# A state-space scan with a wave mixer on one core: u of two adjoining tiles with its tails as 64-row products, token weights loaded as float and cast on chip, and the written order made anew

## The chip, the cores and the metric

The kernel runs on one core of a Trainium2 chip. The metric is the device time of one execution in microseconds (us). The kernel before takes 207.25 us, the median of 3 runs (206.68 to 207.59). A run's time is somewhat longer than the span of its profile, which runs from the first to the last thing the profiler saw.

## The reference

There are two stages. The first is a recurrence over 768 steps for each of 4 batches and 8 heads, with a 40 x 40 state:

```
y[t]   = r[t] @ state
Sa     = state @ a[t]
state  = state * w[t] - outer(Sa, b[t]) + outer(v[t], k[t])
```

The second is a mixer over tokens and channels, with x the result y laid out as (batch, 768 tokens, 320 channels):

```
theta  = x @ w_theta                       # 320 x 320
zr, zi = x * cos(theta), x * sin(theta)
u      = x + w_tok_r @ zr + w_tok_i @ zi   # 768 x 768, over tokens
out    = u + relu(u @ w_ch)                # 320 x 320
```

Inputs and output are float32; the products run in bf16.

## The kernel before, in words

The tokens are cut into 24 tiles of 128 (six for each batch), numbered 0 to 23. The recurrence is done tile by tile in matrix form: within a tile it becomes products of 128 x 128 score matrices, and only the state (`gt`) is carried from tile to tile. The mixer works on the same tiles; the row products of a tile need z of all six tiles of its batch.

Every step of a tile is a short name in one long text, `ORDER`, and the kernel does nothing but walk through it: `LDK:3` issues the load of k of tile 3, `KH:3G` computes its scaled k and b on GpSimd, `PSI:3@0` makes a score matrix on TensorE into bank 0. The letter behind a step is its engine (A is ScalarE or ACT, V is VectorE or DVE, G is GpSimd or POOL, S is a transposing DMA issued by SP). Each engine executes its own steps in the order in which they stand in the text; the scheduler that inserts the waits does not reorder them. The text thus sets which buffer is held when, and what waits behind what on each engine and queue.

The steps that the texts below speak of:

- Loads: `LDW`, `LDK`, `LDB`, `LDA`, `LDV`, `LDR` (w and r come for two tiles at once). Before, k, a, b and v of the first tile or two go to ACT's queue, all others to SP's.
- Decay: `LN` takes the logarithm of w for two tiles. `CSI` and `CSE` sum it over tokens on TensorE, as products of 64 rows with a triangular mask (`pair_inc`, `pair_exc`). `INVW` and `WI` exponentiate the sums on ACT.
- Scaled inputs: `KH` (k and b by invW), `AH` (a by Wi), casts `CR`, `CV`.
- Transposes on TensorE with copies out of PSUM behind them: `TRK`/`EKBT`, `TRA`/`EAT`, `TRV`/`EVT`, `TRR`/`ERT`, `NUT`/`ENUT`, `GD`/`EGD`, `XT`/`EXT`, `UT`/`EUT`. Where the copy has the letter S, a DMA transposes from memory and TensorE does nothing.
- Scores: `PSI`, `PHI`, `LV`, `LU`, each eight products of 64 rows, two heads' halves of the array in turn. `EPSI`, `EPHI`, `ELV`, `ELU` bring them to memory: on DVE with the mask in the same instruction, on ACT without it, and then POOL masks them (`MPSI`, `MPHI`, `MLV`, `MLU`).
- `X0`, `NU`: the corrections. `GT`, `GI`, `EGA`, `EGT`: the new state. `Y`, `EX`: the result x of a tile.
- Mixer: `TH` (x by `wth`), `SIN` on ACT, `ZR` (z of a tile), `YR` (row products, twelve a tile, 320 columns each), `EU` (u), `CH` (u by `wch`), `EO` (result), `ST` (store).
- Weights over tokens: `LDT:t.n` loads 128 rows of one of the two matrices, `WT` transposes them on TensorE, `EWT` copies. `LDC` loads the channel weights.

The 320 channels are contracted in three slices of 128, of which the third holds 64 channels and 64 zeros. x and u lie in tiles of 384 columns padded with zeros for this:

```
    def mix3(dst, lhs, rhs):
        for kt in range(3):
            mm(dst, lhs[:, kt, :], rhs[:, kt, :], kt == 0, kt == 2)
```

The token weights are loaded by POOL's queue into bf16 tiles, with the conversion done by the DMA; three buffers of each matrix.

Of the kernel before, what the change touches and what calls it, by code (L numbers as in the profile page):

```python
# [19 lines left out]
LDW:0 LDK:0A LDB:0 LDA:0A LDA:1 LDB:1A LDK:1 LDV:0A LN:0A LDC:0.0G LDT:0.0G CSI:0@0 LDC:0.1G CSE:0@1 WI:0A  # L20
INVW:0A KH:0V TRK:0@0 AH:0V EKBT:0A TRA:0@3 LDW:2 EAT:0V LDR:0 KH:1V PHI:0@1 PSI:0@0
EPSI:0A MPSI:0G CV:0A LDB:2 EPHI:0A AH:1V TRK:1@1 EKBT:1V LN:2A TRA:1@2 MPHI:0G LDV:1 TRV:0@3
LDK:2 X0:0@0 EAT:1V CSI:2@0 CR:0A ENX:0V LDA:2 PSI:1@1 INVW:2A EVT:0V NU:0 ENU:0A EPSI:1V
TRR:0@1 PHI:1@0 LDB:3 ERT:0A GT:0@2 CV:1A LDK:3 CSE:2@1 EPHI:1V TRV:1@3 ERT:1A NUT:0@0 KH:2G
WI:2A EGT:0V LV:0@0 LDA:3 EVT:1V X0:1@1 ENX:1A ENUT:0A ELV:0V LDV:2 AH:2G GD:0@2 LDR:2 TRK:2@3
KH:3G LV:1@1 NU:1 EKBT:2A LU:0@0 ELV:1V LDW:4 TRA:2@0 ENU:1A LDV:3 ELU:0A NUT:1@3 AH:3G EAT:2V
GT:1@1 ENUT:1V PSI:2@1 TRK:3@0 EGD:0V EPSI:2V LDK:4 LDA:4 GI:1 EKBT:3A CV:2G TRA:3@3 LU:1@0
ELU:1A CR:2G PHI:2@1 EGT:1V X0:2@2 EAT:3V EPHI:2V MLU:0G ENX:2A LN:4A LDB:4 TRR:2@0 PSI:3@0
LDR:4 CV:3G PHI:3@1 MLU:1G Y:0@1 EPSI:3A MPSI:3G EPHI:3V NU:2 TRV:2@3 CSE:4@0 LDV:4 ENU:2A
ERT:2A EVT:2V GT:2@2 EX:0V WI:4A AH:4G CSI:4@1 INVW:4A Y:1@3 LDW:6 NUT:2@1 EGA:2V EGT:2V ERT:3A  # L30
ENUT:2V LV:2@0 LDA:5 TRV:3@2 EX:1V X0:3@1 ELV:2A KH:4G EVT:3V LU:2@1 ENX:3V ELU:2V LV:3@0
TRA:4@0 ELV:3A LDK:5 NU:3 TRK:4@3 LDB:5 GD:1@2 EAT:4V ENU:3A MLV:2G XT:0@0 EKBT:4V CR:4A GT:3@1
GI:3 EGD:1V EGT:3V PSI:4@1 EPSI:4V CV:4G PHI:4@0 LN:6A TRR:4@3 EPHI:4A NUT:3@2 MLV:3G Y:2@1
ENUT:3V LDB:6 LDA:6 AH:5G LDK:6 CSI:6@1 X0:4@2 EX:2V EXT:0A ERT:4A INVW:6A TRV:4@0 ENX:4V
MPHI:4G LDV:5 KH:5G LU:3@0 ERT:5A XT:1@1 NU:4 ELU:3V EXT:1A CSE:6@1 LDV:6 LDT:1.1G ENU:4A
TRA:5@3 WI:6A NUT:4@1 EVT:4V ENUT:4A TRK:5@2 LDK:7 EAT:5V AH:6G XT:2@0 EKBT:5V LV:4@0 TH:0@3
ELV:4V KH:6G PSI:5@1 GD:2@1 LDR:6 SIN:0A TH:1@2 LU:4@0 CV:5G GT:4@3 GI:4 EXT:2A EPSI:5V CV:6G
ZR:0G LDW:8 TRA:6@0 PHI:5@1 LDB:7 ELU:4A LDA:7 EGD:2V EGT:4V TH:2@1 SIN:1A EAT:6V MLU:4G SIN:2A
TRK:6@3 X0:5@0 GD:3@2 EPHI:5V EKBT:6V ENX:5A LDB:8 Y:3@1 ZR:1G EGD:3V EX:3V PSI:6@0 EPSI:6V
TRV:5@3 TRV:6@2 Y:4@1 LN:8A LDK:8 NU:5 PHI:6@1 EVT:6V ENU:5V EVT:5A CR:6G X0:6@2 EPHI:6V  # L40
LDT:1.0G KH:7G TRR:6@0 ENX:6A CSI:8@0 INVW:8A LDA:8 LDV:7 EX:4V NUT:5@3 LV:5@1 ELV:5A LDB:9
ERT:6V AH:7G ENUT:5V TRK:7@1 CSE:8@0 ERT:7V KH:8G TRA:7@3 WI:8A LDV:8 LV:6@1 EAT:7V EKBT:7V
ELV:6A LU:5@0 LDA:9 GD:4@0 NU:6 ELU:5V AH:8G PSI:7@1 TRK:8@3 LDK:9 ENU:6A EGD:4A CV:7A MLV:5G
# [93 lines left out]
def kernel(  # L137
# [247 lines left out]
    def cse(i, b):  # L385
# [448 lines left out]
```

## Time and profile before

| | |
|---|---|
| median of 3 runs | 207.25 us |
| profiled execution | 206.92 us, span 205.2 us |
| granted TensorE clock | 0.999 |
| TensorE busy | 190.1 us (93%), 3266 products and transposes |
| DVE busy | 170.6 us (83%) |
| ACT busy | 154.3 us (75%) |
| POOL busy | 147.1 us (72%) |
| DMA packets | 144802, 34.17 MB, mean 167 GB/s |

The profile gives busy time, idle time with what ended it, the timeline of each engine, and the DMA queues. Matmuls are pipelined: their shown durations overlap, so that the distance from start to start tells what one costs. An engine that is off the bound may idle without cost. Under the table of one stretch "busy (x)" is the busy time and in brackets the number of instructions.

### The profile page before, as it was taken

Reading aid. Unit: us, or ns where it says so; the run is one execution under the profiler, and the core shown is the slowest. Engines: PE = TensorE matmul, PEld = TensorE weight load, DVE = VectorE, ACT = ScalarE, POOL = GpSimd, SP = SyncE. Lnnn points to the kernel's source line nnn. Section 1 sums busy time; section 2 is a strip of 40 time slices with the busy share of each in tenths; the row PEclk is TensorE's granted clock in tenths of the full one; section 3 lists DMA queues with packets and bytes.
Section 4 is the critical chain, followed back from the end, with each engine's and each line's share of the span. In section 5 each row is a group of like instructions: output and inputs, shape, how many; then the busy total and the mean of one; then the engine's idle time right before and its main releaser. Section 6 shows DMA issues by size and latency. Waiting matters only on the chain.

```text
span 205.2 us, 7809 instructions
## 1 busy us (share of the span) xinstructions
PE 190.1 (93%) x3266; PEld 147.5 (72%) x3266; DVE 170.6 (83%) x334; ACT 154.3 (75%) x259; POOL 147.1 (72%) x157
## 2 busy tenths in 40 slices
PE   0389999999999999999999999999999999999992
PEld 0166777877777887887887877887877787777671
DVE  7256899999999997999799998989888797975653
ACT  2367799997989997999899788987898685822100
POOL 8225778899989699998966886993989785634000
PEclk9999999999999999999999999999999999999999
DMA  7999999998898999899489989987979996433342
GB/s 136 187 240 159 225 171 178 173 230 140 153 221 154 213 159 216 164 213 226 103 171 193 192 172 238 192 135 161 169 97 154 218 129 140 99 90 103 102 150 96
DMA packets 144802, 34.17 MB, mean 167 GB/s; under 512 B 139520, under 2 KB 144768, under 8 KB 144768
## 3 DMA queue, kind: packets, MB, share of 16 engines
q1 hardware_dynamic: 138176, 30.26, 76.5%
q0 software_dynamic: 2432, 2.77, 8.4%
q10 hardware_dynamic: 4160, 0.66, 2.2%
q8 instruction: 25, 0.41, 0.9%
q14 instruction: 9, 0.07, 0.1%
HBM read 29.13 MB, written 3.93 MB: 161 GB/s over the span
## 4 chain that ended last, share of the span: by engine, by line
PE 80%; ACT 6%; DVE 5%; issue 2%; ACTq 2%; POOL 2%; POOLq 0%; DVEq 0%
PE sm L278 39%; PE sc L278 22%; PE sm L282 20%; ACTq L331 1%; ACT kbT L270 1%; ACT psi L270 1%; DVE phi L275 1%; ACTq L326 1%; ACT Wi_two L412 1%; ACT lw_two L338 1%; POOL z L275 1%; DVE lamu L275 1%; DVE rvT L272 1%; POOL lamv L554 1%; POOL phi L554 1%
## 5 line engine op out<-in xcount | busy, mean ns | idle before, releaser
L275 POOL TENSOR_TENSOR kb<-raw_kb,invW_two 128x640 bf16<-128x640 f32 x22 | 33.9, 1542 | 5.5 <-ACT invW_two L373 3.6
L275 POOL TENSOR_TENSOR z<-cs,x 128x640 bf16<-128x640 f32 x22 | 30.8, 1403 | 5.3 <-ACT cs L677 5.3
L278 PE MATMUL sm<-z,wtok_r 128*128 128x320 bf16 x120 | 34.3, 299 | 0.0
L278 PE MATMUL sm<-z,wtok_i 128*128 128x320 bf16 x120 | 34.2, 299 | 0.0
L275 POOL TENSOR_TENSOR ah<-raw_a,Wi_two 128x320 bf16<-128x320 f32 x22 | 19.0, 866 | 8.5 <-issue 5.2
L275 DVE TENSOR_TENSOR psi<-sc,mask_p 128x1024 bf16<-128x1024 f32 x16 | 19.5, 1219 | 1.0 <-PE sc L278 0.9
L554 POOL TENSOR_SCALAR_AFFINE_SELECT psi<-psi 128x1024 bf16<-128x1024 bf16 x8 | 8.7, 1093 | 14.0 <-ACT psi L270 11.6
L275 DVE TENSOR_TENSOR phi<-sc,mask_p 128x1024 bf16<-128x1024 f32 x14 | 17.1, 1219 | 1.6 <-PE sc L278 1.4
L278 PE MATMUL sc<-aT,kbT 64*128 64x128 bf16 x384 | 17.3, 225 | 1.1 <-ACT kbT L270 0.7
L275 DVE TENSOR_TENSOR lamu<-sc,mask_p 128x1024 bf16<-128x1024 f32 x14 | 17.1, 1220 | 0.6 <-PE sc L278 0.3
L282 PE MATMUL sm<-ident,kb 128*128 128x128 bf16 x184 | 14.9, 227 | 2.6 <-DVE kb L275 2.3
L278 PEld LDWEIGHTS <-wtok_r 128*128 128x128 bf16 x144 | 14.0, 97 | 4.6 <-issue 0.3
L270 ACT COPY rvT<-sm 128x512 bf16<-128x512 bf16 x28 | 15.9, 593 | 1.3 <-PE sm L282 0.7
L278 PEld LDWEIGHTS <-wtok_i 128*128 128x128 bf16 x144 | 14.1, 98 | 3.9 <-issue 0.2
L275 DVE TENSOR_TENSOR lamv<-sc,mask_p 128x1024 bf16<-128x1024 f32 x13 | 15.9, 1220 | 1.0 <-PE sc L278 0.5
L677 ACT ACTIVATE cs<-sm 128x320 f32<-128x320 f32 x26 | 9.9, 452 | 8.5 <-PE sm L278 8.4
L278 PEld LDWEIGHTS <-kbT 64*128 64x128 bf16 x384 | 11.9, 97 | 5.8 <-issue 2.4
L278 PEld LDWEIGHTS <-rvT 64*128 64x128 bf16 (+1 forms) x272 | 13.6, 95 | 2.9 <-issue 0.5
L278 PE MATMUL sm<-kb,lamv 128*128 128x40 bf16 x192 | 15.0, 180 | 0.0
L278 PE MATMUL sm<-kb,lamu 128*128 128x40 bf16 x192 | 14.9, 179 | 0.0
L282 PEld LDWEIGHTS <-kb 128*128 128x128 bf16 x184 | 11.5, 101 | 4.2 <-DVE kb L275 2.3
L554 POOL TENSOR_SCALAR_AFFINE_SELECT lamu<-lamu 128x1024 bf16<-128x1024 bf16 x10 | 10.9, 1090 | 4.1 <-ACT lamu L270 4.1
(137 smaller groups left out, 625.0 us busy)
## 6 DMA issues: line engine op xcount, KB each, us to landing
raw_w_two<-in_w_dram SPq DMA_DIRECT2D x12, 320.0 KB, 4.8
raw_r_two<-in_r_dram SPq DMA_DIRECT2D x12, 320.0 KB, 4.8
out_dram<-oo SPq DMA_DIRECT2D x24, 160.0 KB, 2.5
raw_kb<-in_b_dram SPq DMA_DIRECT2D x23, 160.0 KB, 4.6
raw_a<-in_a_dram SPq DMA_DIRECT2D x23, 160.0 KB, 4.5
raw_kb<-in_k_dram SPq DMA_DIRECT2D x23, 160.0 KB, 4.3
raw_v<-in_v_dram SPq DMA_DIRECT2D x23, 160.0 KB, 4.7
wtok_row<-in_moe_w_tok_r_dram POOLq DMA_DIRECT2D x6, 192.0 KB, 4.8
```

The lines of the kernel that those rows point to most:

```text
L270: keep(nc.scalar.copy(out=out, in_=in_))
L272: keep(eng[e].tensor_copy(out=out, in_=in_))
L275: keep(eng[e].tensor_tensor(out=out, in0=in0, in1=in1, op=ALU.mult))
L278: keep(nc.tensor.matmul(out, lhsT=lhsT, rhs=rhs, start=start, stop=stop, skip_group_check=True))
L282: keep(nc.tensor.transpose(out=out, in_=in_, identity=ident))
L326: keep(queue[e].dma_start(out=tiles[i].raw_kb[:, j], in_=source(ap, i)))
L331: keep(queue[e].dma_start(out=t, in_=source(ap, i)))
L338: keep(nc.scalar.activation(out=q.lw[:, :, :, 0:D], in_=q.raw_w.rearrange("p h (j d) -> p j h d", j=2), func=AF.Ln))
L412: keep(nc.scalar.activation(out=two, in_=q.cse[:, LO:LO + 2 * DM + 16], func=AF.Exp))
L554: keep(nc.gpsimd.affine_select(out=flat, in_=flat, compare_op=ALU.is_ge, fill=0.0, base=-1, pattern=[[0, 2 * G], [1, 128]], channel_multip ...
L677: keep(nc.scalar.activation(out=cs[i % 5][:, c], in_=tiles[i].theta, func=AF.Sin, bias=(math.pi / 2, 0.0)[c]))
```

## The change

Three things change in the code, and the text `ORDER` is written anew.

1. **u of two tiles in one buffer.** u of an even tile and of the odd tile behind it lie side by side in 640 columns. The even tile transposes its first 256 columns, the odd one the other 384, whose first slice of 128 holds the last 64 channels of the even tile and the first 64 of the odd one. `CH` of either tile does two full products, and a new step `CHR` does two products of 64 rows each, one on either half of the array's rows: the first ends the even tile's sum, the second begins the odd tile's. `wch` has two more slices for that, with the odd tile's channels shifted by 64. x keeps its three slices (`THR`, the same for theta, does not occur in the text).
2. **Token weights as float.** `LDT` is issued by SP and brings float32 rows into one buffer for each matrix; a new step `CW` casts them to bf16 on POOL (ten times) or ACT (twice).
3. **Smaller things.** The totals that `CSE` made behind its sums are a step of their own, `CST`. All loads go to SP's queue. theta has three buffers instead of four.

The core of the diff:

```diff
-        q.u = u_t[i % 3][:, 0:DM]
+        q.u, q.usrc = home(i, twin_u, u_t, u_two)
...
+    def home(i, twins, one, two):
+        if i not in twins:
+            t = one[i % len(one)]
+            return t[:, 0:DM], t
+        t = two[i // 2 % len(two)]
+        if i % 2:
+            return t[:, DM:2 * DM], t[:, 256:2 * DM]
+        return t[:, 0:DM], t[:, 0:256]
...
-        q.ops = bank(b)
-        mix3(q.ops[:, 0:DM], q.uT, wch)
+        mix(i, b, "ops", q.uT, wch, twin_u)
...
+        elif i % 2 == 0:
+            setattr(q, name, bank(b))
+            for kt in range(2):
+                mm(getattr(q, name)[:, 0:DM], lhs[:, kt, :], rhs[:, kt, :], kt == 0, False)
+        else:
+            for kt in range(2):
+                mm(getattr(q, name)[:, 0:DM], lhs[:, 1 + kt, :], rhs[:, 3 + kt, :], False, kt == 1)
+
+    def mix_ends(i, b, name, lhs, rhs):
+        setattr(tiles[i], name, bank(b))
+        for c in range(2):
+            mm(getattr(tiles[i - 1 + c], name)[:, 0:DM], lhs[rows(c), 0, :], rhs[rows(c), 2, :],
+               c == 1, c == 0)
...
-        wrows[tb, n] = tile_of(wrow, [128, S], BF16, f"wtok_row_{n}")
-        keep(nc.gpsimd.dma_start(out=wrows[tb, n],
-                                 in_=moe_w_tok[n][tb * 128:(tb + 1) * 128, :]))
+        wrows[tb, n] = tile_of(wraw, [128, S], FP32, f"wtok_raw_{n}")
+        keep(nc.sync.dma_start(out=wrows[tb, n], in_=moe_w_tok[n][tb * 128:(tb + 1) * 128, :]))
+
+    def row_cast(tb, n, e):
+        t = tile_of(wrow, [128, S], BF16, f"wtok_row_{n}")
+        copy(e, t, wrows[tb, n])
+        wrows[tb, n] = t
...
-LDW:0 LDK:0A LDB:0 LDA:0A LDA:1 LDB:1A LDK:1 LDV:0A LN:0A LDC:0.0G LDT:0.0G CSI:0@0 LDC:0.1G CSE:0@1 WI:0A
+LDW:0 LDW:2 LDC:0.2G LDB:0 LDK:0 LDC:0.0G LDA:0 LN:0A LDB:1 CSI:0@0 CSE:0@1 LDK:1 INVW:0A CST:0
```

What the new text does to the engines' lists is shown at three places. First ACT at the start of the program, before (lw_two is the logarithm, Wi_two and invW_two the exponentials, psi and phi scores of tile 0):

```order
L326 DMA raw_kb<-in_k_dram 128x8x40
L331 DMA raw_a<-in_a_dram 128x8x40
L326 DMA raw_kb<-in_b_dram 128x8x40
L331 DMA raw_v<-in_v_dram 128x8x40
L338 ACTIVATE lw_two_93<-raw_w_two 128x16x40
L412 ACTIVATE Wi_two<-sc_237 128x656
L373 ACTIVATE invW_two<-sc_231 128x640
L270 COPY kbT<-sm_256 128x1024
L270 CAST psi<-sc_289 128x1024
L270 CAST v_103<-raw_v 128x8x40
L270 CAST phi<-sc_280 128x1024
L338 ACTIVATE lw_two_94<-raw_w_two 128x16x40
```

and the same place of the changed kernel:

```order
L359 ACTIVATE lw_two_93<-raw_w_two 128x16x40
L394 ACTIVATE invW_two<-sc_221 128x640
L359 ACTIVATE lw_two_94<-raw_w_two 128x16x40
L436 ACTIVATE Wi_two<-sc_226 128x656
L394 ACTIVATE invW_two<-sc_251 128x640
L436 ACTIVATE Wi_two<-sc_244 128x656
L291 COPY aT<-sm_288 128x512
L291 CAST v_103<-raw_v 128x8x40
L291 CAST phi<-sc_307 128x1024
```

The four loads have left ACT, the first invW stands ahead of Wi, the second logarithm has moved from the eighth compute step to the third, and the copy of kbT and the score psi of tile 0 are no longer ACT's.

Second, POOL's list in the middle of the program, around the scaled k and b (kb) of tile 10, before (wtok_row is a bf16 token load, z_204 the z of the first batch):

```order
L723 DMA wtok_row_1759<-in_moe_w_tok_i_dram 128x768
L723 DMA wtok_row_1775<-in_moe_w_tok_i_dram 128x768
L275 TENSOR_TENSOR z_204<-cs_199,x_116 128x640
L275 TENSOR_TENSOR kb_99<-raw_kb,invW_two 128x16x40
L275 TENSOR_TENSOR ah_95<-raw_a,Wi_two 128x8x40
```

and of the changed kernel, where raw_1467, 1563 and 1706 are the float rows:

```order
L293 CAST wtok_row_1673<-wtok_raw_1467 128x768
L578 AFFINE_SELECT lamv<-lamv 128x1024
L293 CAST wtok_row_1732<-wtok_raw_1563 128x768
L293 CAST v_104<-raw_v 128x8x40
L296 TENSOR_TENSOR z_198<-cs_193,x_two_113 128x640
L293 CAST wtok_row_1812<-wtok_raw_1706 128x768
L296 TENSOR_TENSOR kb_99<-raw_kb,invW_two 128x16x40
```

The loads have gone and three casts stand ahead of kb of tile 10. On SP the loads of that place now read (raw_kb from b and raw_a are those of tile 10):

```order
L352 DMA raw_v<-in_v_dram 128x8x40
L762 DMA wtok_raw_1706<-in_moe_w_tok_r_dram 128x768
L347 DMA raw_kb<-in_b_dram 128x8x40
L762 DMA wtok_raw_1766<-in_moe_w_tok_i_dram 128x768
L352 DMA raw_a<-in_a_dram 128x8x40
L327 DMA raw_r_two<-in_r_dram 128x8x80
L762 DMA wtok_raw_1853<-in_moe_w_tok_r_dram 128x768
```

Each token load of this piece waits until the cast of the row before it has freed the one buffer of its matrix, and the loads behind it wait with it.

Third, TensorE's list where u of tiles 0 and 1 is multiplied by the channel weights (sm0_2895 and sm2_2901 are the two results, uT_2807 and uT_2854 the transposed u of tile 0 and of tile 1). Rows between are left out, before:

```order
L282 MATMUL sm3_2641<-ident_58,gt_0_109 128x128
L278 LDWEIGHTS uT_2637
L278 MATMUL sm1_2648<-wch_207,uT_2637 128x320
...
L282 LDWEIGHTS wtok_row_1_2346
L282 MATMUL sm2_2652<-ident_58,wtok_row_1_2346 128x128
```

and of the changed kernel:

```order
L299 MATMUL sm0_2895<-wch_201,uT_2807 128x320
L299 LDWEIGHTS uT_2854
L299 MATMUL sm0_2895<-wch_201,uT_2854 128x320
...
L299 MATMUL sm2_2901<-wch_201,uT_2854 128x320
L299 LDWEIGHTS nuT_2856
L299 MATMUL sc0_2904<-rvT_2629,nuT_2856 128x128
...
L299 LDWEIGHTS rvT_2827
L299 MATMUL sc1_2915<-rvT_2827 128x128
...
L299 LDWEIGHTS uT_2854
L299 MATMUL sm2_2901<-wch_201,uT_2854 128x320
```

Before, three full products of tile 0 stand between other full products. Now the 64-row pair (the second and third product of the piece) is followed by the sixteen 64-row products of two score matrices, and the full products of tile 1 come behind them. Seven of the twelve pairs stand beside such products in the new list, five stand between full products.

335 lines of the change are left out of this document (179 added, 156 removed).

## The prediction

> **What bounds the kernel now.** I read the page first, its busy shares and the 40 slices.
>
> ```profile
> PE 190.1 (93%) x3266; PEld 147.5 (72%) x3266; DVE 170.6 (83%) x334; ACT 154.3 (75%) x259; POOL 147.1 (72%) x157
> PE   0389999999999999999999999999999999999992
> DVE  7256899999999997999799998989888797975653
> DMA  7999999998898999899489989987979996433342
> ```
>
> TensorE is busy 93% of 205.2 us, but a slice with a 9 does not yet say that it works at its peak. The table by stretches, cut where the x of tile 8 is written (near 80), shows three stages.
>
> ```profile
> core 0: us, PE busy (x) PEld busy (x) DVE busy (x) ACT busy (x) POOL busy (x), PEclk, DMA share, GB/s
> 0.00:20.00 20.00, 10.29 (x117) 7.59 (x117) 10.87 (x56) 10.36 (x15) 9.24 (x20) 1.00 1.13 184
> 20.00:80.00 60.00, 58.47 (x1188) 45.80 (x1184) 56.19 (x93) 54.65 (x92) 52.92 (x55) 1.00 1.00 185
> 80.00:199.50 119.50, 119.27 (x1955) 93.14 (x1952) 101.26 (x181) 88.85 (x152) 84.94 (x83) 1.00 0.81 158
> 154.50:186.20 31.70, 31.65 (x509) 24.16 (x507) 25.75 (x47) 20.41 (x35) 22.02 (x21) 1.00 0.69 135
> ```
>
> In 0 to 20 us every engine is half idle while the DMA engines are full (share 1.13). In 20 to 80 nothing has room: DVE 94%, ACT 91%, POOL 88%, DMA 1.00. From 80 to 199.5 TensorE alone is full (119.27 of 119.50). So a microsecond saved early is kept only if the whole pack moves up, and after 80 us what counts is TensorE's list, how long it is and whether anything makes it wait. Its prices come from the timeline.
>
> ```profile
> 183.00 0.57 PE L278 MATMUL sm<-wth,xT 128*128 128x320 bf16 x3
> 183.50 0.40 PE L278 MATMUL sc<-rvT,nuT 64*128 64x128 bf16 x8
> 183.83 0.31 PE L278 MATMUL sm<-z,wtok_r 128*128 128x320 bf16 x1
> 183.97 0.30 PE L278 MATMUL sm<-z,wtok_i 128*128 128x320 bf16 x1
> ```
>
> Durations of 0.3 us overlap, so starts are what to read: a 320-column product takes 0.14 us (183.83 to 183.97). Three of them should end at 183.42, but the 64-row group starts at 183.50: 0.08 lost on the way in. Its eight products run two at a time on the two row halves; four pairs at 0.055 (what a full 128-column product takes, next fence) are 0.22, yet 0.33 pass until the next full product: 0.11 lost on the way out. **Each group of 64-row products costs 0.19 us beside its work.**
>
> ```profile
> 199.35 0.30 PE L278 MATMUL sm<-z,wtok_i 128*128 128x320 bf16 x1
> 199.49 0.33 PE L282 MATMUL sm<-ident,u 128*128 128x128 bf16 x3
> 199.65 0.57 PE L278 MATMUL sm<-wch,uT 128*128 128x320 bf16 x3
> 201.69 0.49 DVE L715 SCALAR_TENSOR_TENSOR oo<-sm,u 128x320 f32<-128x320 f32 x1
> ```
>
> Three transposes take 0.16 us here (199.49 to 199.65), 0.055 each. The last row product ends at 199.49 and the last result at 202.18, 2.69 us later; the store fills the span to 205.2.
>
> **The change, part by part.** The profiled execution took 206.92 us, 1.72 more than its span, and lies 0.33 below the median of the runs, 207.25. The sum is made against 206.92; 0.3 goes on at the end.
>
> *u in pairs.* Twelve pairs of tiles lose their two padded thirds, 24 products of 0.14 (3.36 us), and gain two 64-row products each, in different row halves. If they run together a pair costs one full product, 0.14, 1.68 in all: net -1.68. If they did not, 0.28 a pair: 0.0. I take the first, since the 64-row rows above run in twos. All of them stand behind the x of tile 8 in the list, so all of it lies in TensorE's full stage. The Trainium skill, "TensorEngine Tiling (Array Packing)", Tiling Modes, Key Properties, speaks against the change here: going from one tiling mode to another drains TensorE; the trace agrees, with 0.08 and 0.11 us. By that rule alone twelve pairs would give back 2.3 us and the pairs would lose 0.6. Counted in the new order, seven of the twelve stand next to score products or sums of logs, which are 64-row already, and five stand alone.
>
> *Mode changes.* Before, the list has 84 groups of 64-row products, now 72, the five lone pairs among them: 12 x 0.19 = 2.3 us less. All of it lies ahead of the Y of tile 8 (44 groups there become 32); behind it there are 40 and 40, so the lone pairs are paid for by scores that were put together. In the early stage TensorE is one of five things that are nearly full, so between 0 and 2.3 us of this reaches the end. I take 0.4, near zero, because DVE and the DMA stay as they were.
>
> *Other products.* Transposes by letters of the two lists: x 9 fewer, u 1 more (an odd tile still has three), nu 8, v 4, gd 4 and token rows 6 more: 14 x 0.055 = +0.77. Two more products that carry the old state: +0.28. TensorE's full stage thus changes by -1.68 + 0.77 + 0.28 = -0.6.
>
> *The start.*
>
> ```profile
> 6.20 0.72 PE L278 MATMUL sc<-lw_two,pair_inc 64*128 64x320 bf16 x4 [6.20 <-ACT lw_two L338]
> 7.83 0.72 ACT L412 ACTIVATE Wi_two<-sc 128x656 f32<-128x656 f32 x1 [1.68 <-PE sc L278]
> 8.44 0.70 ACT L373 ACTIVATE invW_two<-sc 128x640 f32<-128x640 f32 x1
> 9.17 0.83 DVE L275 TENSOR_TENSOR kb<-raw_kb,invW_two 128x640 bf16<-128x640 f32 x1 [3.76 <-ACT invW_two L373]
> 13.20 1.10 SPq L326 DMA_DIRECT2D raw_kb<-in_k_dram  x1
> 13.27 1.01 ACT L270 CAST psi<-sc 128x1024 bf16<-128x1024 f32 x1 [1.13 <-PE sc L278]
> 14.36 1.08 POOL L554 TENSOR_SCALAR_AFFINE_SELECT psi<-psi 128x1024 bf16<-128x1024 bf16 x1 [8.13 <-ACT psi L270]
> 15.44 0.75 ACT L338 ACTIVATE lw_two<-raw_w_two 128x640 bf16<-128x640 f32 x1
> 15.50 0.45 PE L278 MATMUL sm<-v,psi 128*128 128x40 bf16 x8 [0.20 <-POOL psi L554]
> 17.78 1.54 POOL L275 TENSOR_TENSOR kb<-raw_kb,invW_two 128x640 bf16<-128x640 f32 x1 [1.07 <-ACT invW_two L373]
> ...
> L275 DVE TENSOR_TENSOR psi<-sc,mask_p 128x1024 bf16<-128x1024 f32 x16 | 19.5, 1219 | 1.0 <-PE sc L278 0.9
> ```
>
> invW of tile 0 now stands ahead of Wi, so it can follow its sums at 6.92 instead of 8.44: 1.5 us for kb. psi of tile 0 goes to DVE with its mask (1.22) instead of ACT and POOL (13.27 to 15.44, 2.17): 0.9 more. The second log, at 15.44 the eighth instruction of ACT, is now its third. That makes X0 of tile 0 some 2.4 us earlier. But the DMA engines are full, so loads set what is kept.
>
> ```profile
> q1 hardware_dynamic: 138176, 30.26, 76.5%
> q0 software_dynamic: 2432, 2.77, 8.4%
> raw_kb<-in_k_dram SPq DMA_DIRECT2D x23, 160.0 KB, 4.3
> wtok_row<-in_moe_w_tok_r_dram POOLq DMA_DIRECT2D x6, 192.0 KB, 4.8
> ```
>
> A packet of the first queue holds an engine 0.765 x 205.2 x 16 / 138176 = 18 ns; 160 KB in 160-byte pieces are 64 packets an engine, 1.16 us. The software queue's packets hold 113 ns by the same working, 0.9 us for the eight an engine of a 128-row token load. Tile 2 waits for its k (issued 13.20, kb at 17.78). In the new order r of tile 0 (as many packets as a load, 1.16 at the least), v of tile 1 and one token load (0.9) no longer stand ahead of the k and b of tile 2, and its a does: 2.1 us net; ahead of the k and b of tile 3 only the token load is gone, 0.9. The two theta loads stay; the log weights of tiles 2 and 3 now go ahead of b and k of tile 0, a delay of 1.16 that the 1.5 us of waiting there covers about. I take -1.8 for the start, between 0.9 and 2.4.
>
> *Token weights.*
>
> ```profile
> L272 POOL CAST v<-raw_v 128x320 bf16<-128x320 f32 x15 | 6.8, 453 | 0.1
> L272 POOL CAST r<-raw_r_two 128x640 bf16<-128x640 f32 x7 | 5.0, 720 | 0.0
> L723 POOL DMA_DIRECT2D wtok_row<-in_moe_w_tok_r_dram x6 | 3.5, 580 | 0.0
> ```
>
> Twelve issues of 0.58 us leave POOL; ten casts come, by the two sizes above 0.83 us each for 768 columns (estimate), and two go to ACT: POOL +1.3. As float the same 128 rows are 3 KB packets; with no row for that size I bound a load by 0.9 us (as now) and twice that, and the share of 0.81 after 80 us hides either. The raw row has one buffer, so ten of the twelve loads must wait on SP until POOL or ACT has cast the row before, and all loads behind stand still meanwhile (rival below). Cost taken: 0.
>
> *End.* The last two results both come behind the last 64-row pair now, so that one result (0.49, the row at 201.69) stands between it and the end that had its own place before, while TensorE has one product (0.14) less for that pair: between -0.14 and +0.49. I take +0.1, nearer to zero, as the copies of u that the end waits for are now shared by two engines.
>
> Sum: -1.8 - 0.4 - 0.6 + 0.1 = -2.7, so 204.2 in the terms of the profiled run and 204.5 as a median. Its own bounds: -0.9 - 0 - 0.6 + 0.1 = -1.4 (205.8) to -2.4 - 2.3 - 0.6 = -5.3 (201.9).
>
> **Rivals.**
>
> *The early gain is lost on the way.* If the re-made middle leaves TensorE 2.2 us of waits that it has not now (0.23 us in 119.5), only -0.6 + 0.1 stays: 206.7. For it: the middle is as re-made as the start. Against: lists of equal work kept it full before.
>
> *POOL becomes the bound near the end (slower).* Between the x of tile 18 (154.5) and of 23 (186.2):
>
> ```profile
> L275 POOL TENSOR_TENSOR z<-cs,x 128x640 bf16<-128x640 f32 x7 | 9.7, 1403 | 5.1 <-ACT cs L677 5.1
> L554 POOL TENSOR_SCALAR_AFFINE_SELECT lamu<-lamu 128x1024 bf16<-128x1024 bf16 x3 | 3.3, 1091 | 2.4 <-ACT lamu L270 2.3
> L275 POOL TENSOR_TENSOR ah<-raw_a,Wi_two 128x320 bf16<-128x320 f32 x3 | 2.6, 861 | 1.5 <-issue 1.5
> ```
>
> The new list has 25 POOL entries there instead of 17: masks 3 more net (3.3 us), z 2 (2.8), ah 1 (0.9), v 2 (0.9): +7.9 on 22.0, 29.9 of 31.7. POOL decides once more than 1.8 us of waits stay. If the 5.1 for ACT's sines stay, the stretch grows by 3.3; with the 2.4 for lamu, by 5.7: 207.8 to 210.2, say 209.0. Against it: TensorE has row products of other tiles in store, which wait for none of this.
>
> *SP's queue stands still (slower).* From the cast that frees the row to kb of tile 10 POOL has 4.6 us of work (one mask, two casts of rows, one v, one z); a load issued then needs 4.3 to 4.8 to land plus about 0.5 to issue. If POOL loses 0.45 at each of the ten, +4.5: 209.0. It decides where a load lands over 4.6 us after that cast. Against: a queue that has stood still is short, and loads then land sooner.
>
> *The 64-row pairs do not run together.* Then +1.7: 206.2.
>
> **How the numbers follow.** Forecast 0.55; early gain lost 0.15; POOL 0.17; SP 0.09; pairs not together 0.04. A measurement of this kernel can tell about 0.5%, 1.04 us, from no change: under 206.2 is faster, over 208.3 slower. The forecast lies under it in all its bounds, the first and last rival are the same, POOL and SP are slower: 0.55, 0.19, 0.26. The range from 201.9 to 209.2 leaves out the upper half of the two slow rivals (0.13) and a little below (0.05).
>
> **What would show it.** Right: kb of tile 0 starts near 7.7, X0 of tile 0 near 13, kb of tile 2 before 16.5; the x of tile 8 near 75.5; TensorE's busy time in the following 110 us still over 99%; the two products of a pair start within 0.01 us of each other; 2.8 us from the last row product to the last result. Wrong: a wait of TensorE on POOL in the last 50 us (POOL rival); SP's waits on POOL at token loads followed by waits on raw_kb landings (SP rival); x of tile 8 early but the end not (first rival).

## The result, and the profile after

The changed kernel takes 208.01 us, the median of 20 runs (206.67 to 209.37); the kernel before took 207.66 (206.62 to 210.12) on the same chip. The ratio is 1.0008, with a 95% interval from 0.999 to 1.0027: no difference. The forecast was 204.5. The profiled execution has a span of 205.5 us where the kernel before had 205.2.

The page of the changed kernel, its busy shares and two rows of the 40 slices:

```profile
PE 188.2 (92%) x3282; PEld 146.6 (71%) x3282; DVE 169.6 (83%) x339; ACT 156.3 (76%) x254; POOL 156.4 (76%) x163
...
PE   0887999999999799999999999999999898999992
...
DMA  6999999899999999999967989796995996533413
```

TensorE is busy 1.9 us less and still ends no earlier. The table by stretches, with the columns of the one before, tells where:

```profile
0.00:20.00 20.00, 12.66 (x186) 9.54 (x187) 13.99 (x57) 12.70 (x19) 9.84 (x21) 1.00 1.04 177
20.00:80.00 60.00, 56.66 (x1164) 45.16 (x1164) 54.92 (x93) 55.04 (x92) 54.68 (x56) 1.00 0.98 200
80.00:199.50 119.50, 117.03 (x1924) 91.20 (x1921) 98.49 (x186) 88.20 (x145) 91.86 (x88) 1.00 0.82 165
...
154.50:186.20 31.70, 30.29 (x491) 23.28 (x488) 21.34 (x41) 21.96 (x36) 25.80 (x24) 1.00 0.64 120
```

In the first 20 us TensorE is busy 2.4 us longer than before (12.66 against 10.29): the start is earlier, as forecast. From 80 to 199.5 us it is busy 117.03 of 119.50; before it was 119.27. The stage that had no idle time has 2.2 us more of it now.

The steps of the start, in the timeline:

```profile
7.34 0.82 DVE L296 TENSOR_TENSOR kb<-raw_kb,invW_two 128x640 bf16<-128x640 f32 x1 [2.05 <-DMA raw_kb<-in_k_dram]
12.91 0.45 PE L299 MATMUL sm<-v,psi 128*128 128x40 bf16 x8
15.36 1.54 POOL L296 TENSOR_TENSOR kb<-raw_kb,invW_two 128x640 bf16<-128x640 f32 x1
75.39 0.48 DVE L296 TENSOR_TENSOR x_two<-sm,Wi_two 128x320 bf16<-128x320 f32 x1
```

The x of tile 8 in the kernel before:

```profile
77.58 0.48 DVE L275 TENSOR_TENSOR x<-sm,Wi_two 128x320 bf16<-128x320 f32 x1
```

kb of tile 0 (forecast 7.7), X0 of tile 0 (forecast 13), kb of tile 2 (forecast ahead of 16.5) and x of tile 8 (forecast 75.5) all come when they were to come.

I then priced TensorE's whole list by starts: 0.136 us for a product of 320 columns, 0.056 for one of 128, 0.025 to 0.036 for smaller ones, and 0.094 for each change between 128-row and 64-row products (a full product of 320 columns starts 0.232 before its successor where that is a 64-row one, and a 64-row one of 320 columns 0.228 before a full one, instead of 0.136). What a stretch has beyond that is waiting:

| us | before: products, changes, waiting | after: products, changes, waiting |
|---|---|---|
| 0 to 20 | 4.9, 8, 14.3 | 7.5, 9, 11.7 |
| 20 to 80 | 46.8, 82, 5.5 | 46.9, 60, 7.4 |
| 80 to 160 | 72.8, 63, 1.3 | 72.1, 52, 3.0 |
| 160 to 185 | 23.5, 14, 0.2 | 21.9, 12, 2.0 |
| 185 to the end | 15.8, 0, 4.4 | 14.8, 10, 4.7 |

Work fell by 0.6 us, 24 changes fewer are 2.3, the start waits 2.6 less: 5.5 us gained. Waiting behind 20 us grew by 1.9 + 1.7 + 1.8 + 0.3 = 5.7. The whole gain was turned into waits. A second profile of the same kernel (experiment 8) gives by the same prices 11.7, 6.9, 3.6, 2.0 and 4.9 us of waiting, so this is not the chance of one execution. From 80 to 185 us the waits of over 0.15 us stand at eight places and add up to 3.6 us; in the kernel before there is one such place, with 0.3. Three of the single ones, the first ahead of 80 us, with the ACT rows that make the second:

```profile
67.86 0.51 PE L303 MATMUL sm<-ident,kb 128*128 128x128 bf16 x6 [1.07 <-POOL kb L296]
...
162.20 1.28 ACT L717 ACT_TABLE_LOAD   x1 [1.20 <-PE sm L299]
163.49 0.77 ACT L717 ACTIVATE cs<-sm 128x320 f32<-128x320 f32 x2
164.31 0.20 PE L299 MATMUL sm<-gd,rvT 128*128 128x80 bf16 x1 [0.83 <-ACT cs L717]
170.94 0.40 PE L299 MATMUL sc<-rvT 64*128 64x128 bf16 x8 [0.58 <-DVE rvT L293]
```

At 164.31 Y of tile 20 needs bank 3 of PSUM, which holds theta of tile 17 until ACT's two sines have read it, and ACT must first load their table. By starts TensorE loses 0.99 there. At 170.94 the scores of tile 22 wait (0.65 by starts) for rT of tile 22, which was placed behind rT of tile 23. The list of TensorE's waits from 80 to 199.5 us says the same; for the kernel before it is empty:

```profile
PE sm L299 <- ACT cs L717: 0.8, 1, 0.8
PE sc L299 <- DVE rvT L293: 0.6, 1, 0.6
PE sm L303 <- DVE rvT L293: 0.4, 2, 0.3
PE sm L303 <- POOL kb L296: 0.3, 1, 0.3
```

The end, in the timeline:

```profile
198.78 0.30 PE L299 MATMUL sm<-z,wtok_i 128*128 128x320 bf16 x1
...
200.31 0.37 ACT L291 COPY uT<-sm 128x256 bf16<-128x256 bf16 x1 [8.76 <-PE sm L299]
200.74 1.07 PE L299 MATMUL sm<-wch,uT 128*128 128x320 bf16 x6 [0.46 <-ACT uT L291]
201.46 0.89 DVE L754 SCALAR_TENSOR_TENSOR oo<-sm,u_two 128x320 f32<-128x320 f32 x2 [0.66 <-PE sm L299]
```

The last row product ends at 198.91, the last result at 202.35: 3.44 us, where the kernel before took 2.69.

### The profile page after: what moved, and what is told of

It reads as the page before. It is cut to its first block, busy times and chain, and to the rows that moved or that the text cites. A ratio compares the mean times of both kernels' runs of the same rounds, so it can differ in the third digit from the quotient of the medians.

```text
span 205.5 us, 7850 instructions
## 1 busy us (share of the span) xinstructions
PE 188.2 (92%) x3282; PEld 146.6 (71%) x3282; DVE 169.6 (83%) x339; ACT 156.3 (76%) x254; POOL 156.4 (76%) x163
## 4 chain that ended last, share of the span: by engine, by line
PE 61%; ACT 13%; SPq 8%; DMA 8%; DVE 4%; issue 2%; POOL 2%; DVEq 0%; POOLq 0%; ACTq 0%
PE sm L299 32%; PE sm L303 14%; PE sc L299 14%; DMA raw_kb<-in_b_dram 5%; SPq L347 4%; DMA raw_w_two<-in_w_dram 3%; ACT cs L717 2%; POOL kb L296 2%; SPq L352 2%; DVE rvT L293 2%; ACT L717 2%; ACT kbT L291 1%; ACT L319 1%; ACT rvT L291 1%; SPq L341 1%
## 5 line engine op out<-in xcount | busy, mean ns | idle before, releaser
L296 POOL TENSOR_TENSOR z<-cs,x_two 128x640 bf16<-128x640 f32 x23 | 32.1, 1403 | 6.5 <-ACT cs L717 6.5
L296 DVE TENSOR_TENSOR psi<-sc,mask_p 128x1024 bf16<-128x1024 f32 x17 | 20.7, 1216 | 0.7 <-PE sc L299 0.6
L578 POOL TENSOR_SCALAR_AFFINE_SELECT lamu<-lamu 128x1024 bf16<-128x1024 bf16 x14 | 15.3, 1093 | 4.0 <-ACT lamu L291 4.0
L296 DVE TENSOR_TENSOR phi<-sc,mask_p 128x1024 bf16<-128x1024 f32 x15 | 18.3, 1217 | 0.1
L291 ACT CAST lamu<-sc 128x1024 bf16<-128x1024 f32 x14 | 14.2, 1012 | 5.3 <-PE sc L299 5.3
L578 POOL TENSOR_SCALAR_AFFINE_SELECT phi<-phi 128x1024 bf16<-128x1024 bf16 x9 | 9.8, 1090 | 9.7 <-ACT phi L291 9.6
L578 POOL TENSOR_SCALAR_AFFINE_SELECT lamv<-lamv 128x1024 bf16<-128x1024 bf16 x14 | 15.3, 1094 | 1.0 <-ACT lamv L291 1.0
L754 DVE SCALAR_TENSOR_TENSOR oo<-sm,u_two 128x320 f32<-128x320 f32 x24 | 11.1, 484 | 5.5 <-PE sm L299 5.2
L293 DVE COPY rvT<-sm 128x512 bf16<-128x512 bf16 x27 | 14.3, 542 | 1.1 <-ACT rvT L291 1.0
L291 ACT CAST lamv<-sc 128x1024 bf16<-128x1024 f32 x14 | 14.3, 1019 | 1.0 <-PE sc L299 1.0
```

The costliest lines, as they stand in the source:

```text
L291: keep(nc.scalar.copy(out=out, in_=in_))
L293: keep(eng[e].tensor_copy(out=out, in_=in_))
L296: keep(eng[e].tensor_tensor(out=out, in0=in0, in1=in1, op=ALU.mult))
L578: keep(nc.gpsimd.affine_select(out=flat, in_=flat, compare_op=ALU.is_ge, fill=0.0, base=-1, pattern=[[0, 2 * G], [1, 128]], channel_multip ...
L754: keep(nc.vector.scalar_tensor_tensor(out=q.oo, in0=q.ops[:, 0:DM], scalar=0.0, in1=q.u, op0=ALU.max, op1=ALU.add))
```

## The experiments

**Theory A**: the lead of the start is real; it is eaten by single waits of TensorE that the re-made order plants behind it, of several kinds. **B**: SP's queue stands still at the token loads, or POOL's casts cost. **C**: the pairs of u eat what they save. **D**: loads and the other engines set the pace up to 80 us whatever the start does. **F**: a wait that is mended late comes back as another. Ratios are to the kernel before, timed in the same rounds; 1% is 2.07 us.

**1. Token loads back on POOL's queue.**

```diff
-        wrows[tb, n] = tile_of(wraw, [128, S], FP32, f"wtok_raw_{n}")
-        keep(nc.sync.dma_start(out=wrows[tb, n], in_=moe_w_tok[n][tb * 128:(tb + 1) * 128, :]))
+        wrows[tb, n] = tile_of(wrow, [128, S], BF16, f"wtok_row_{n}")   # three buffers
+        keep(nc.gpsimd.dma_start(out=wrows[tb, n], in_=moe_w_tok[n][tb * 128:(tb + 1) * 128, :]))
```

> The changed kernel with its twelve token loads put back on POOL's queue, converted by the DMA, three bf16 buffers of each matrix and no casts on chip; everything else as in the changed kernel. Theory A (the early lead is lost in single waits that the new order plants in the middle, at places of many kinds): two or three of the waits of TensorE on kb between 60 and 125 us shrink, together 1 us or less, so 207.0 to 208.0. Rival B (SP's queue stands still at the token loads, and ten casts of 0.83 us delay POOL's kb): the waits of TensorE between 60 and 125 us fall by 2 us or more, 206.0 or below. If the issues on POOL (0.58 each) cost as much as the casts: 208 to 208.5.

Measured 0.9963 (0.993 to 0.9995), median 206.68: 0.8 to 0.9 us less than the changed kernel. That lies between what A (207.0 to 208.0) and B (206.0 or below) had forecast. TensorE's wait for kb of tile 10, 1.21 us by starts at 67.86 in the changed kernel, is not there any more:

```profile
67.61 0.62 PE L297 MATMUL sm<-ident,kb 128*128 128x128 bf16 x8
```

So the mechanism of B is there, at a small price. In the changed kernel, from 55 to 112 us, the longest of SP's waits at the token loads (L762), in us in total, times, longest:

```profile
SPq L762 <- POOL wtok_row L293: 2.3, 3, 0.9
SPq L762 <- POOL v L293: 1.6, 1, 1.6
SPq L762 <- POOL kb L296: 1.0, 1, 1.0
```

With the smaller ones they add up to 6.8 us. POOL then waits for landings (55 to 125 us):

```profile
POOL wtok_row L293 <- DMA wtok_raw<-in_moe_w_tok_r_dram: 1.1, 1, 1.1
POOL kb L296 <- DMA raw_kb<-in_b_dram: 1.0, 1, 1.0
...
POOL kb L296 <- DMA raw_kb<-in_k_dram: 0.2, 1, 0.2
```

In the experiment's trace POOL waits for no landing at all in that stretch. But the kernel before, whose token loads are on POOL's queue too, does, and for as long:

```profile
POOL kb L275 <- DMA raw_kb<-in_b_dram: 1.7, 1, 1.7
...
POOL ah L275 <- DMA raw_kb<-in_b_dram: 0.5, 1, 0.5
```

Waits of POOL for landings alone thus don't tell the two ways of loading apart.

**2. No pairs of u.**

```diff
-CH:0@0 ... CHR:1@2 ... CH:1
+CH:0@0 ... CH:1@2          # three products and three transposes for each tile
```

> The changed kernel with u in one buffer for each tile again (384 columns, six buffers), three full products and three transposes for each tile where the pair's last product stood, and no 64-row products of u; the order is otherwise that of the changed kernel. Theory A: TensorE has 12 products of 0.14 and 12 transposes of 0.055 more and up to five lone mode changes of 0.19 fewer, +2.3 - 0.9 = +1.4 us, 209.0 to 209.8. Rival C (the pairs tie two tiles together and their waits and mode changes eat what they save): no slower than the changed kernel, 207.4 to 208.2.

Measured 1.0048 (1.0017 to 1.008), median 208.45: 0.8 to 1.0 us slower than the changed kernel. By the price list it has 2.1 us more products and 10 changes (0.9) fewer, 1.1 in all. Theory A had forecast 1.0 to 1.8 us over the changed kernel, C none. The pairs are worth a little less than the list says; C falls, though the difference is only just clear of noise. That their two products run together shows in the changed kernel's timeline, where the two of a pair and the sixteen scores behind them follow at once:

```profile
164.94 0.31 PE L299 MATMUL sm<-wch,uT 64*128 64x320 bf16 x2
165.09 0.61 PE L299 MATMUL sc<-aT,kbT 64*128 64x128 bf16 x16
```

**3 and 4. The start a little later, and a little earlier.**

```diff
-INVW:0A CST:0 LN:2A CSE:2@0 WI:0A     (changed kernel)
+CST:0 LN:2A CSE:2@0 WI:0A INVW:0A
-WI:0A INVW:0A                         (kernel before)
+INVW:0A WI:0A
```

> The changed kernel with invW of tile 0 put back behind Wi of tiles 0 and 1 on ACT, so that kb, X0 and x of tile 0 come 1 us or more later. Theory A: the lead of the start is carried through the middle and eaten by waits that do not depend on it, so its loss shows at the end, +0.7 to +1.5 us: 208.7 to 209.5. Rival D (loads or other queues set the pace of the middle whatever the start does): the same time as the changed kernel within 0.4 us, 207.6 to 208.4.

> The kernel before with one step moved: invW of tile 0 ahead of Wi on ACT, which brings kb of tile 0 about 1.5 us earlier. Theory A: the kernel before has TensorE full from 80 us on, so an earlier start reaches the end in part: 0.5 to 1.5 us faster, 206.2 to 207.2. Rival D: the loads set the pace up to 80 us, no change within 0.4 us, 207.3 to 208.1.

Measured 0.9995 (0.997 to 1.002) and 0.9996 (0.9969 to 1.0023): inconclusive. The first moved kb of tile 0 by only 0.5 us, and x of tile 1 not at all. In the second the x of tiles 0 and 8 come 0.8 us earlier and the profiled spans differ by 0.6 (204.6, 205.2), but over all runs the two kernels are alike, within some 0.6 us either way: the 0.5 to 1.5 us that theory A forecast did not show. A larger step was needed.

**11 and 12. The start held back by some 2 us, in both kernels.**

```diff
+IDLE:4A                               # four copies of 128x640 on ACT
 INVW:0A                               # in the kernel before: ahead of WI:0A
```

> The changed kernel with four copies of 128x640 (0.7 us each, of a zeroed buffer onto itself) on ACT ahead of invW of tile 0: the start is held back by some 2 us (kb of tile 0 at 9 to 10 instead of 7.3), nothing else is changed. If the lead of the start is real and is carried to 80 us and beyond: 1.2 to 2.2 us more, 208.9 to 209.9. If loads and the other engines set the pace up to 80 us whatever the start does (rival D, and then the forecast's term of -1.8 was wrong by itself): under 0.6 more, 207.5 to 208.3.

> The kernel before with the same four copies on ACT ahead of Wi of tile 0, so that its start comes some 2 us later still. If an early microsecond is carried through its middle: 1.2 to 2.2 us more, 208.8 to 209.8. Rival D: under 0.6 more, up to 208.2.

The changed kernel held back, kb of tile 0 and x of tile 8:

```profile
9.96 0.82 DVE L292 TENSOR_TENSOR kb<-raw_kb,invW_two 128x640 bf16<-128x640 f32 x1 [3.66 <-ACT invW_two L394]
...
76.78 0.48 DVE L292 TENSOR_TENSOR x_two<-sm,Wi_two 128x320 bf16<-128x320 f32 x1
```

The kernel before held back, the same:

```profile
11.02 0.83 DVE L270 TENSOR_TENSOR kb<-raw_kb,invW_two 128x640 bf16<-128x640 f32 x1 [4.27 <-ACT invW_two L372]
...
79.57 0.48 DVE L270 TENSOR_TENSOR x<-sm,Wi_two 128x320 bf16<-128x320 f32 x1
```

Measured 1.008 (1.0052 to 1.0108) and 1.0099 (1.0065 to 1.0132). In the changed kernel 2.6 us at kb are 1.4 at the x of tile 8 (1.9 against the profile of experiment 8, where it comes at 74.85) and 1.5 to 1.7 at the end; in the kernel before 1.9 at kb are 2.0 at x of tile 8 and 2.0 at the end. What is late at tile 8 is late at the end by about as much, in either order, and D, which allowed under 0.6, falls. That a lead is carried like a delay is inferred from this: experiment 4, which made one, did not show it clear of noise.

**5. The two late waits, first try.**

```diff
-TH:17@3 ... SIN:17A EAT:22V           ERT:23A ERT:22V
+TH:17@3 ... ETH:17V SIN:17A EAT:22V   ERT:22A ERT:23A
```

> The changed kernel with its two longest waits of TensorE after 130 us taken away by order: theta of tile 17 is copied out of PSUM by DVE, so that bank 3 is free for Y of tile 20 before ACT's sines (wait of 0.99 us at 164.3), and rT of tile 22 is copied ahead of that of tile 23, by ACT (wait of 0.65 us at 170.9). Theory A (TensorE's list sets the time after 80 us, each wait in it reaches the end): 1.3 to 1.7 us less than the changed kernel, 206.0 to 206.6. Rival F (the chain of states from tile to tile sets the pace there, and what is gained comes back as another wait before 185 us): less than 0.5 us, 207.2 to 207.8.

Measured 0.9985 (0.9955 to 1.0015): little or nothing, as F says. Kernel 7, which has the same edit, shows the reason:

```profile
166.86 0.40 PE L293 MATMUL sc<-aT,kbT 64*128 64x128 bf16 x8 [1.24 <-ACT lamv L285]
```

The copy put ACT's sines later, the cast of lamv stood behind them, and a score bank came free 1.40 us late.

**9. The two late waits again.**

```diff
-SIN:17A EAT:22V ... ELV:21A ENU:21V ZR:17G ... EPSI:22A MLV:21G ... MPSI:22G
+EAT:22V ETH:17V ... ELV:21A SIN:17A ENU:21V ... EPSI:22V MLV:21G ZR:17G
-ERT:23A ERT:22V
+ERT:22A ERT:23A
```

> The changed kernel with the two late waits mended in another way, since the first try put ACT's sines later and TensorE then waited 1.40 us for a score bank: lamv of tile 21 goes ahead of the sines of tile 17 on ACT, theta of tile 17 is copied out by DVE, psi of tile 22 is masked by DVE (no mask on POOL for it), z of tile 17 goes behind the mask of lamv on POOL, rT of tile 22 ahead of that of 23 on ACT. Theory A (TensorE's list sets the time after 80 us): 0.8 to 1.5 us less than the changed kernel, 206.2 to 206.9. Rival F (the engines behind the scores set the pace there and a wait comes back): within 0.4 of it, 207.3 to 207.9.

Measured 0.9971 (0.9935 to 1.0007), median 207.02; the changed kernel, run again as experiment 8, had 1.0. The row of 160 to 185 us, in the kernel before, the changed kernel and this one (one fence each):

```profile
160.00:185.00 25.00, 25.00 (x409) 19.19 (x407) 21.34 (x38) 15.41 (x27) 16.52 (x15) 1.00 0.65 130
```

```profile
160.00:185.00 25.00, 23.59 (x386) 18.35 (x384) 16.34 (x31) 16.94 (x29) 19.50 (x19) 1.00 0.71 126
```

```profile
160.00:185.00 25.00, 24.64 (x388) 18.67 (x385) 17.11 (x33) 16.50 (x28) 19.14 (x18) 1.00 0.70 126
```

TensorE wins back 1.05 of the 1.41 us it had lost. About 0.6 of it shows in the ratio, inside an interval that also holds none.

**6, 7 and 8. Three waits in the middle, everything together, and the changed kernel again.**

```diff
-EUT:2S CW:5.0G ... LDB:17             (experiment 6; 7 has 1 and 5 as well)
+CW:5.0G ... LDB:17 EUT:2S
-TRK:10@1 ENUT:8V NU:9 WI:10A WT:1.1@3
+ENUT:8V NU:9 WI:10A WT:1.1@3 TRK:10@1
-UT:7@0 LV:18@1
+LV:18@1 UT:7@0
```

> The changed kernel with three waits in the middle eased by order: the transposing DMA of u of tile 2 on SP's queue goes behind the loads of k and b of tile 17 instead of ahead of them (it holds the queue for 2.1 us, kb of tile 17 then waits 1.0 on a landing, TensorE 0.5 at 121.4), the transposes of kb of tile 10 go behind those of a token row (wait of 1.21 at 67.9), the transposes of u of tile 7 behind a score (0.33 at 138.9). Theory A: 1.0 to 1.8 us less than the changed kernel, 206.0 to 206.8. Rival D (loads and the other engines set the pace up to 120 us): the wait at 67.9 comes back elsewhere, 0.3 to 0.7 us less, 207.0 to 207.5.

> The changed kernel with the edits of the two runs before and with the token loads on POOL's queue as in the first experiment (207.5 becomes 206.6 by that alone). Theory A: the three sums add up, 0.9 + 1.5 + 1.2 = 3.6 us less than the changed kernel, 203.8 to 204.8, which is about what was forecast. Rivals D and F: 0.9 to 1.8 less, 205.8 to 206.8.

> The changed kernel itself, on the same chip as the three others, so that they can be set against it: 207.3 to 208.0, within 0.3% of the kernel before.

Measured 1.0132 (1.0084 to 1.018), 1.0021 (0.9989 to 1.0054) and 1.0 (0.9976 to 1.0023). Experiment 6 missed both forecasts (0.3 to 1.8 us less) by a wait that its own edit planted, and that wait shows A better than the experiment was meant to. The transposing DMA that I moved brings u that `CH:2` needs:

```profile
118.51 0.71 PE L295 MATMUL sm<-wch,uT 128*128 128x320 bf16 x2 [2.44 <-DMA uT<-u_two]
```

x of tile 13 comes at 111.1 (0.9 earlier than in the changed kernel of experiment 8), x of tile 14 at 122.7 (2.5 later). One wait of 2.60 us at 118.5 makes tile 14 2.5 us late, and the kernel ends 2.7 us late: what is lost in the middle is not made good.

Experiment 7, forecast at 203.8 to 204.8 by A and 205.8 to 206.8 by its rivals, missed both with a median of 208.5. It can't tell whether gains add up, since its edits planted two waits: the 1.40 us of experiment 5, and 1.05 by starts where the transposes of the token row, now ahead of those of kb of tile 10, wait for their own load:

```profile
68.34 0.45 PE L297 MATMUL sm<-ident,wtok_row 128*128 128x128 bf16 x5 [0.89 <-DMA wtok_row<-in_moe_w_tok_i_dram]
```

**10 and 13. The useful edits together.** Experiment 10 is 9 with 1 and the step of `UT:7`; 13 has one load moved as well.

```diff
-LDK:23 EX:20V ... EXT:18S ... LDA:23
+LDK:23 LDA:23 EX:20V ... EXT:18S
```

> The changed kernel with the edits of the run before, the token loads on POOL's queue as in the first experiment, and the transposes of u of tile 7 behind a score. Theory A: the gains add up, 0.9 + 1.2 + 0.2 = 2.3 us less than the changed kernel, 205.2 to 205.8, faster than both kernels. Rival F: the gain of the first experiment alone, 206.5 to 206.9.

> The kernel of the run with token loads by POOL and the late waits mended, with the load of a of tile 23 moved ahead of three transposing DMAs on SP's queue: in that run it landed behind them, POOL waited 2.12 us for it and TensorE 0.83 for the transposes of a at 172.2. Theory A (every wait of TensorE after 80 us reaches the end): 0.5 to 0.9 less than that run, 205.6 to 206.3, faster than both kernels. Rival F (another wait takes its place): 206.6 to 207.0.

Measured 0.9984 (0.9952 to 1.0016) and 0.9966 (0.9931 to 1.0002). In 10 a new wait had come, POOL's for a of tile 23 (TensorE lost 0.83 by it at 172.2). SP's queue and POOL in that kernel:

```profile
160.07 2.37 SPq L466 DMA_TRANSPOSE gdx<-gt  x1
...
166.69 0.56 SPq L346 DMA_DIRECT2D raw_a<-in_a_dram  x1
...
171.30 0.86 POOL L290 TENSOR_TENSOR ah<-raw_a,Wi_two 128x320 bf16<-128x320 f32 x1 [2.12 <-DMA raw_a<-in_a_dram]
```

The transposing DMA of the state held the queue for 2.37 us (1.45 in kernel 9), and the load, behind it and two more of them, was issued 0.94 later than there. With that gone, 13 has the next one, at the transposed x that another such DMA brings (0.73 by starts):

```profile
189.78 0.58 PE L293 MATMUL sm<-wth,xT 128*128 128x320 bf16 x3 [0.56 <-DMA xT<-x_two]
```

So the gains don't add up: A's 205.2 to 205.8 for 10 did not come, 13 shows 0.4 us of the 0.5 to 0.9 forecast for it, inside the noise, and neither kernel is faster than that of experiment 1 alone (0.9963). F holds for a part of them.

**14 and 15. Casts twice; float loads by POOL.**

```diff
         copy(e, t, wrows[tb, n])
+        if e == "G":
+            copy(e, t, t)                    # experiment 14
-        keep(nc.sync.dma_start(out=wrows[tb, n], in_=moe_w_tok[n][tb * 128:(tb + 1) * 128, :]))
+        keep(nc.gpsimd.dma_start(out=wrows[tb, n], in_=moe_w_tok[n][tb * 128:(tb + 1) * 128, :]))   # 15
```

> The changed kernel in which each of POOL's ten casts of a token row is followed by a copy of the bf16 row onto itself (0.5 to 0.9 us each, estimate by the cast's 0.83), which does not hold the float row. If the work of the casts on POOL is what the token weights cost: 0.6 to 1.5 us more than the changed kernel, 208.2 to 209.2. If it is SP's queue standing still (rival B in its narrow form): under 0.4 more, 207.4 to 208.1.

> The changed kernel with its float token loads issued by POOL's queue instead of SP's, casts kept, so that SP's queue never waits for a cast; POOL has twelve issues of about 0.58 us more. If SP's queue standing still is what the token weights cost: 0.4 to 1.0 less than the changed kernel, 206.7 to 207.3, in spite of the issues. If POOL's time is: 0.5 to 1.5 more, 208.2 to 209.2.

Experiment 14 measured 1.0141 (1.0098 to 1.0184), by these groups of POOL:

```profile
L293 POOL COPY wtok_row<-wtok_row 128x768 bf16<-128x768 bf16 x10 | 8.3, 827 | 0.6
L293 POOL CAST wtok_row<-wtok_raw 128x768 bf16<-128x768 f32 x10 | 8.3, 826 | 0.0
```

8.3 us more on POOL cost 2.9, more than either side had forecast: POOL is close to a bound there, busy 55.60 of the 57 us from 55 to 112 where the changed kernel has 50.98. The copy also stands between a row's cast and its transposes, so this is not the price of work on POOL alone. Experiment 15 measured 1.0396 (1.0348 to 1.0444), 8.2 us and again outside both forecasts. It doesn't separate what it was to separate: POOL issues a load only where its list has it, and then waits for the landing itself. POOL's waits, 55 to 125 us:

```profile
POOL wtok_row L293 <- DMA wtok_raw<-in_moe_w_tok_r_dram: 4.3, 2, 3.0
POOL wtok_row L293 <- DMA wtok_raw<-in_moe_w_tok_i_dram: 2.5, 2, 1.8
```

The two together say that the token stage has little room on POOL. How the 0.9 us of experiment 1 divide between SP's waits and POOL's casts stays open.

**16 and 17. A third buffer of the transposed u**, in the changed kernel and in kernel 13.

```diff
-        t = tile_of(xp, [128, 3, 128], BF16, tag)
+        t = xp.tile([128, 3, 128], BF16, name=tag, tag=tag, bufs=3 if tag == "uT" else 2)
```

> The changed kernel with three buffers instead of two for the transposed u. At the end ACT's copy of u of tile 22 has to wait until the products of tile 21 have read its buffer (copy at 200.31, last products at 200.74, 3.44 us from the last row product to the last result where the kernel before takes 2.69). Theory A with an end that was priced too low (the forecast had +0.1, the profile shows +0.75): the wait of 0.6 before the last products goes, 0.3 to 0.5 us less than the changed kernel, 207.2 to 207.5, and 2.9 to 3.1 us behind the last row product. Rival (the copies on DVE set the end): no change, 207.5 to 208.0.

> The same third buffer in the kernel with token loads by POOL, the late waits mended and the load of a of tile 23 moved. Theory A: 0.3 to 0.5 less than that kernel's 0.9966 of the kernel before, 0.993 to 0.996, faster than both. Rival: as that kernel, 0.996 to 0.998.

Measured 0.9999 (0.9962 to 1.0037), inconclusive, and 0.9959 (0.9925 to 0.9993). The end of kernel 17:

```profile
199.46 1.50 PE L293 MATMUL sm<-wch,uT 128*128 128x320 bf16 x8
199.46 0.37 ACT L285 COPY uT<-sm 128x256 bf16<-128x256 bf16 x1 [8.50 <-PE sm L297]
...
200.61 0.89 DVE L748 SCALAR_TENSOR_TENSOR oo<-sm,u_two 128x320 f32<-128x320 f32 x2 [0.19 <-PE sm L293]
```

TensorE no longer pauses ahead of the last products; the last result comes 2.97 us behind the last row product instead of 3.44. By its ratio this version is 0.4% faster than the kernel before, and than the changed kernel by about as much, but its interval only just leaves out none, the medians (207.36 and 207.64) differ by less, and it doesn't tell theory A (0.993 to 0.996) from its rival (0.996 to 0.998). By the price list it still waits 2.5 us more behind 80 us than the kernel before. That is spread over places of under 0.5 us, and what ends the waits there was not followed.

## Why the prediction was wrong

- **Start, -1.8: right**, as far as it can be told from the next term: the two add up to 2.2, and the x of tile 8 comes 2.2 us earlier (2.7 in the profile of experiment 8). The held-back starts show that a delay at that place is carried to the end in both kernels.
- **Mode changes, -0.4: right as counted, the size not shown by itself.** Twelve groups fewer, all ahead of Y of tile 8, as counted; from 20 to 80 us they saved 2.1 us of TensorE, and waiting grew there by 1.9, so that about as little was kept as was taken. The Trainium skill, "TensorEngine Tiling (Array Packing)", Tiling Modes, Key Properties, says that a change of mode drains TensorE; the trace agrees, with 0.094 us each way.
- **Products, -0.6: right** by the price list (163.8 to 163.2); experiment 2 agrees for the pairs, with 0.8 to 1.0 us where the list says 1.1.
- **Token weights, 0: wrong by 0.8 to 0.9** (experiment 1). The rival to the step "Cost taken: 0" named SP's waits at the token loads, and they are there (6.8 us), but it was priced all or nothing: 4.5 us, or none. Which part of the change costs the 0.9, SP's waits or POOL's casts, is not shown.
- **End, +0.1: wrong in the profile, +0.75**, above its own bound of +0.49. It counted results and products and took the copies as shared. Two buffers of the transposed u made one copy wait for products; 0.47 of it goes with a third buffer. Whether that alone moves the end, experiment 16 could not tell.
- **The step that failed** is the one that carried the forecast into the sum: that TensorE's list stays full behind 80 us, because "lists of equal work kept it full before". That was an argument from the kernel before about an order that was written anew. Waiting behind 80 us grew from 5.9 to 9.7 us (10.5 in the profile of experiment 8). So the first rival came true, with 3.8 us of waits instead of the 2.2 it was priced at, and with the mark the forecast named for it: x of tile 8 early, the end not. The two largest, 0.99 and 0.65, could have been seen in the order: who holds bank 3, and which of two copies comes first. What makes these two waits, the one on kb of tile 10 and the one at the end, the experiments show, since each goes with its edit. The other waits are measured, but what makes each of them stays open: the best version still has 2.5 us more of them behind 80 us than the kernel before.
- **POOL as the bound near the end** didn't come: in the last 50 us TensorE has no wait on it. Between the x of tile 18 (151.7) and of tile 23 (185.2) POOL is busy 27.60 of 33.50 us, where the rival had 29.9 of 31.7. **64-row pairs apart** didn't either.

## What to carry to other kernels

An engine that is busy 99.8% of a stage, as TensorE was here, leaves a new order of its list nothing to win by filling gaps, and the waits that the order plants can only lose. Before counting work, walk down its new list and ask for each instruction who held its bank and its buffer last, and what stands ahead of that holder on its own engine. To learn whether an early gain is worth anything, hold the start back by a known amount and see how much reaches the end; that prices a delay, and a lead only by inference. One mended wait tends to uncover the next, so sum such gains with a discount.

## What was not expected of the hardware

- A transposing DMA holds SP's queue for 1.2 us at best and at times for twice as long: of the 22 in the changed kernel's trace twelve took 1.17 to 1.22 us, the longest 2.51. That of the state of tile 21 took 1.20 in kernel 9 and 2.42 in kernel 10, where the load behind it was issued at 170.44 instead of 168.66.
- POOL copies 768 columns from bf16 to bf16 no faster (0.827 us) than from float to bf16 (0.826).
- ACT loads the table for the sines (1.28 us) only when their input is there: at 162.20 the load itself waits for TensorE, while ACT had been idle for 1.20 us.
